# Local attention and gated experts on one core: the mask added in PSUM for the first eight pairs, exponentials slot by slot, and a new list of due times

## The chip, the cores and the metric

One Trainium2 chip (trn2), one core of it. The metric is the device time of one execution in microseconds: the median over several executions. The profile is that of one more execution, taken by the hardware profiler.

## The reference, cut to what matters

Eight batches, eight heads, 576 positions, 64 per head. The first four heads see the last 32 positions, the other four every fourth of the last 128. Attention's result, heads side by side, goes through a product with a gate in between.

```python
scores = scale * np.matmul(q, k.transpose(0, 1, 3, 2))
scores = np.where(masks[None], scores, -1e9)
scores = scores - np.max(scores, axis=-1, keepdims=True)
attn = np.exp(scores)
attn = attn / (np.sum(attn, axis=-1, keepdims=True) + 1e-09)
x = np.matmul(attn, v)                       # then (B, S, 512)
h = np.maximum(x @ w_in, 0.0)                # (B, S, 1024)
gate = sigmoid(conv over 3 positions of h, per channel)
out = (h * gate) @ w_out                     # (B, S, 512)
```

## The kernel before, in words

**The work.** `attention(b, p)` (line 228) treats one pair of heads p of batch b: four pairs per batch, pairs 0 and 1 with the plain window (kind 0), 2 and 3 with the dilated one (kind 1). `expert(b, ...)` (line 352) is the rest of a batch: a first product of 16 units (eight blocks of 128 channels by two halves of 288 positions), a gate per block, and a second product of eight units. Every value that goes into these products is split into a high and a low part, both rounded to the type that TensorE multiplies at its full rate (names ending in a and b), so each product is three matmuls per block. `weights` (line 423) brings w_in, w_out and the convolution's weights from 64-bit words in memory to float32 and splits them: a load, one ScalarE step, four VectorE steps; for the first ten blocks (`SUMMED`) three TensorE matmuls and two ScalarE copies do the sum and the split, for the others VectorE does.

**One pair.** A q/k load (line 235) and a v load (line 237) on SP's queue. The scores (lines 243 to 249) are many small matmuls into the PSUM tile `att`: nine slots of 64 keys for 128 rows, slots 0 to 3 in one bank, 4 to 7 in the next, 8 in a third. VectorE adds the mask, reading PSUM, in two pieces (lines 254 and 257); takes the maximum of each slot (260); subtracts it (262). ScalarE takes the exponential of all 576 columns at once (264). VectorE sums (266), adds 1e-9 (268), takes the reciprocal (270), multiplies (271) and transposes in blocks of 32 (273). TensorE multiplies by v (lines 275 to 301), into `att` again. ScalarE copies the result twice, a short and a long piece, as the high part of x (line 330). The low part comes in one of two ways. For the first `HELPED` = 2 batches `less` (lines 334 to 340) lets TensorE subtract the high part from `att`, six matmuls with minus the identity, and ScalarE copies what is left (line 343). In all other batches VectorE subtracts (line 345).

**Buffers.** Line 191 to 193: `att` has one buffer of four banks, used in turn by scores and by value products of all pairs; `mm` and `nn` have two of one bank each. There are two buffers of q/k, three of v, three of s, m and z, two of pt, seven of x.

**The order.** Nothing is issued in program order. Each step is a task with an engine, a cost, a due time and the tasks it waits for (`plan.add`). `Planner.order` (line 113) simulates the engines with these costs: of all tasks that could start within 0.25 us of the first possible start on an engine, the one with the earliest due time goes first; a buffer is given to the task that begins to use it, and free again after its last user. The tasks are written out in the order of the planned starts, and every engine, SP's queue included, runs its own in that order. The due times are numbers by hand (lines 196 to 203): `DUE` for a batch's first product, gates and second product, `PAIR` for its pairs, `AHEAD` for how long before its step a q/k, v or weight load is due:

```python
DUE = {0: (-9.2, 2.8, 30.4), 1: (64.7, 50.1, 92.3)}
PAIR = {0: (-26.0, -24.7, -23.0, -27.0), 1: (-4.9, 1.3, 8.9, 14.5)}
AHEAD = (9.1, 0.8, 0.7)
```

In batch 0 the first product's matmuls of pair k need only the x of pair k, and its units take turns in `mm` and `nn`; in every other batch they need all four pairs (line 369).

**Before the list.** The kinds of masks are loaded on ScalarE's queue (line 475). Identity and its negative are made (476, 477), and VectorE copies the kinds into `mask_sb`, one table of 576 columns per kind (lines 482 to 486, the five copies).

Of the kernel before, what the change touches and what calls it, by code (L numbers as in the profile page):

```python
# [36 lines left out]
BF16 = mybir.dt.bfloat16  # L37
I32 = mybir.dt.int32
U32 = mybir.dt.uint32
AF = mybir.ActivationFunctionType  # L40
ALU = mybir.AluOpType
AX = mybir.AxisListType

B, H, S, D = 8, 8, 576, 64
DM, DF = 512, 1024
NP = 4
NB = 18
W = 64
# [6 lines left out]
SCALE = 1.0 / D ** 0.5  # L55
# [102 lines left out]
def attn_moe(ctx: ExitStack, tc: tile.TileContext, qk_p, qk_d, v_p, v_d, w_in, w_out, conv, mask, out):  # L158
    nc = tc.nc
    const = ctx.enter_context(tc.tile_pool(name="const", bufs=1))  # L160
    psum = ctx.enter_context(tc.tile_pool(name="psum", bufs=1, space=bass.MemoryType.PSUM))

    mask_sb = const.tile([128, 2, 9 * W], BF16, name="mask_sb")
    kinds_sb = const.tile([128, 5, W], BF16, name="kinds_sb")
    conv_sb = const.tile([128, 3, NF], F32, name="conv_sb")
    ident = const.tile([128, 128], F32, name="ident")
    minus = const.tile([128, 128], F32R, name="minus")
    wi = [[const.tile([128, 512], F32R, name=f"wi{j}{c}") for c in range(NF)] for j in range(2)]
    wo = [[const.tile([128, 512], F32R, name=f"wo{j}{c}") for c in range(2 * NC)] for j in range(2)]
    plan = Planner()  # L170
# [24 lines left out]

    DUE = {0: (-9.2, 2.8, 30.4), 1: (64.7, 50.1, 92.3)}
    PAIR = {0: (-26.0, -24.7, -23.0, -27.0), 1: (-4.9, 1.3, 8.9, 14.5)}
    WI, WO = (-20.4, -20.4, -7.2, -7.2, -3.1, -0.1, 7.8, 7.8), (17.2, 17.2, 36.3, 36.3, 36.9, 34.9, 43.2, 43.2)
    AHEAD = (9.1, 0.8, 0.7)
    PERIOD = 55.1  # L200
    for b in range(2, B):
        DUE[b] = tuple(t + PERIOD * b for t in (-5.1, 5.4, 33.0))
        PAIR[b] = tuple(t + PERIOD * b for t in (-21.7, -18.8, -17.2, -13.1))
    SUMMED = 10
    HELPED = 2

# [21 lines left out]
    def attention(b, p):  # L228
        due = PAIR[b][p]
        kind = p // 2  # L230
        qk, v, s, m, z, pt, x = (Buffer(n) for n in ("qk", "v", "s", "m", "z", "pt", "x"))
        sc, tv = Buffer("att"), Buffer("att")
        xs[b, p] = x
        n = (S + KP, QD + KD)[kind]
        lq = plan.add("SP", n * 0.0017, due - AHEAD[0], lambda: nc.sync.dma_start(
# [4 lines left out]
        def scores():  # L240


            for n in [4 * t + i for i in range(4) for t in range(4)] + [16, 17]:
                for hd in range(2):
                    slot, quad = place(hd, n)
                    parts = queries(p, qk.t, hd, n)
                    for i, (q, k) in enumerate(parts):
                        nc.tensor.matmul(sc.t[quad * 32:quad * 32 + 32, slot // 4, slot % 4 * W:slot % 4 * W + W], q, k,  # L248
                                         start=i == 0, stop=i == len(parts) - 1, skip_group_check=True)

        last = plan.add("PE", (0.8, 0.92)[kind], due, scores, [lq], [qk, sc, s], "S")
        flat = lambda: s.t.rearrange("p a k -> p (a k)")
        halves = lambda t: t.rearrange("p (h k) -> p h k", h=2)
        last = plan.add("DVE", 0.68, due + 1.5, lambda: nc.vector.tensor_tensor(  # L254
            out=halves(flat()[:, 0:512]), in0=sc.t[:, 0:2, 0:256], in1=halves(mask_sb[:, kind, 0:512]), op=ALU.add),
            [last], [sc, s])
        last = plan.add("DVE", 0.215, due + 1.5, lambda: nc.vector.tensor_tensor(  # L257
            out=flat()[:, 512:576], in0=sc.t[:, 2, 0:W], in1=mask_sb[:, kind, 512:576], op=ALU.add), [last], [sc, s])
        wide = lambda t: t.unsqueeze(2).to_broadcast([128, 9, W])
        last = plan.add("DVE", 0.755, due + 2.0, lambda: nc.vector.tensor_reduce(  # L260
            out=m.t, in_=s.t, axis=AX.X, op=ALU.max), [last], [s, m])
        last = plan.add("DVE", 0.755, due + 2.5, lambda: nc.vector.tensor_tensor(  # L262
            out=s.t, in0=s.t, in1=wide(m.t), op=ALU.subtract), [last], [s, m])
        last = plan.add("ACT", 0.685, due + 3.0, lambda: nc.scalar.activation(
            out=s.t, in_=s.t, func=AF.Exp, scale=SCALE), [last], [s], "exp")
        last = plan.add("DVE", 0.755, due + 3.5, lambda: nc.vector.tensor_reduce(
            out=z.t, in_=s.t, axis=AX.X, op=ALU.add), [last], [s, z])
        last = plan.add("DVE", 0.173, due + 3.6, lambda: nc.vector.tensor_scalar(
# [33 lines left out]

        last = plan.add("PE", (0.9, 0.85)[kind], due + 6.0, values, [lv, last], [v, pt, tv, x], "V")

# [171 lines left out]
    make_identity(nc, ident)  # L476
    nc.scalar.mul(out=minus, in_=ident, mul=-1.0)


    spread = lambda i, n: kinds_sb[:, i, :].unsqueeze(1).to_broadcast([128, n, W])  # L480
    slot_masks = [mask_sb[:, kind, :].rearrange("p (a k) -> p a k", k=W) for kind in range(2)]
    nc.vector.tensor_copy(out=slot_masks[0], in_=spread(2, 9))
    nc.vector.tensor_copy(out=slot_masks[0][:, 0:5:4, :], in_=kinds_sb[:, 0:2, :])
    nc.vector.tensor_copy(out=slot_masks[1], in_=spread(2, 9))
    nc.vector.tensor_copy(out=slot_masks[1][:, 0:5:4, :], in_=spread(3, 2))
    nc.vector.tensor_copy(out=slot_masks[1][:, 8, :], in_=kinds_sb[:, 4, :])
    for h, in hs:
# [89 lines left out]
```

## Time and profile before

| | |
|---|---|
| median of 3 runs | 549.02 us (548.75 to 549.81) |
| the profiled execution's own time | 548.65 us |
| its span, first to last instruction | 546.9 us |
| TensorE busy, its weight loads | 520.8 us, 496.5 us |
| VectorE busy | 410.0 us |
| ScalarE busy | 289.7 us |
| moved by DMA | 52.32 MB |

The profile names the engines PE (TensorE), PEld (TensorE's weight loads), DVE (VectorE), ACT (ScalarE), POOL (GpSimd) and SP (the queue of loads and stores). L254 is line 254. Matmuls overlap in the pipeline, so the length of one is more than the distance to the next. An instruction's wait is put down to the event that came last. The chain of waits that ended last has, in shares of the span, 88% TensorE, 8% VectorE, 2% ScalarE, 2% DMA.

### The profile page before, as it was taken

The numbers are of one execution on the slowest core, as the hardware profiler recorded it, in microseconds if no ns is written. First come the engines' busy times: TensorE is split into PE (matmuls) and PEld (weight loads), VectorE is DVE, ScalarE is ACT, GpSimd is POOL, SyncE is SP. The second block draws the span as 40 slices with busy tenths as digits, with TensorE's granted clock in tenths as the row PEclk, the third lists the DMA queues.
The fourth block names the chain that finished last, engine by engine and source line by source line (L and its number), as shares of the span: only waits on it lengthen the run. The fifth ranks groups of instructions, "written<-read, shape, count | busy, mean of one in ns | idle before, by whom it ended". The sixth has DMA issues, their size and how long they took to land.

```text
span 546.9 us, 19084 instructions
## 1 busy us (share of the span) xinstructions
PE 520.8 (95%) x8664; PEld 496.5 (91%) x8664; DVE 410.0 (75%) x695; ACT 289.7 (53%) x556; POOL 0.9 (0%) x12
## 2 busy tenths in 40 slices
PE   3599978999999999999999999999999999999997
PEld 2578877999999999999999999999989999999997
DVE  5978999899996389937997399837987289936910
ACT  2466775755742586227742586227732486327721
POOL 0000000000000000000000000000000000000000
PEclk9999997999999999999999999999999999999999
DMA  7765614331135003530144103530045102300011
GB/s 251 267 196 177 207 42 155 100 121 44 50 99 162 18 23 109 163 104 23 52 146 150 30 23 96 170 111 23 28 146 168 35 23 65 112 26 23 0 44 45
DMA packets 17073, 52.32 MB, mean 96 GB/s; under 512 B 2016, under 2 KB 3168, under 8 KB 16992
## 3 DMA queue, kind: packets, MB, share of 16 engines
q1 hardware_dynamic: 16848, 51.02, 28.4%
q8 instruction: 68, 1.11, 0.9%
q10 hardware_dynamic: 144, 0.08, 0.1%
q14 instruction: 13, 0.11, 0.1%
HBM read 41.66 MB, written 9.44 MB: 93 GB/s over the span
## 4 chain that ended last, share of the span: by engine, by line
PE 88%; DVE 8%; ACT 2%; DMA 2%; issue 1%; DVEq 0%; ACTq 0%
PE nn L405 38%; PE mm L363 33%; PE att L283 8%; PE att L248 5%; DVE c L375 2%; PE nn L460 1%; DMA qk<-in_qk_d_dram 1%; PE att L337 1%; DVE s L254 1%; DVE s L262 1%; DVE c L388 1%; DVE m L260 1%; DMA qk<-in_qk_p_dram 1%; DVE pt L273 1%; DVE s L271 1%
## 5 line engine op out<-in xcount | busy, mean ns | idle before, releaser
L375 DVE SCALAR_TENSOR_TENSOR c<-h,conv_sb,c 128x576 f32<-128x576 f32 x128 | 104.0, 815 | 53.2 <-ACT c L381 51.6
L370 ACT ACTIVATE h<-mm 128x288 f32<-128x288 f32 x120 | 48.8, 408 | 49.7 <-PE mm L363 49.5
L412 ACT COPY out<-nn 128x288 f32<-128x288 f32 x64 | 25.3, 397 | 76.4 <-PE nn L405 70.9
L283 PEld LDWEIGHTS att<-pt,v 32*64 32x64 f32 x3072 | 41.4, 140 | 14.8 <-DVE s L257 4.6
L388 DVE TENSOR_TENSOR c<-c,h 128x576 f32<-128x576 f32 x64 | 47.6, 755 | 9.2 <-ACT c L386 7.7
L283 PE MATMUL att<-pt,v 32*64 32x64 f32 (+2 forms) x3072 | 44.9, 234 | 9.3 <-DVE s L257 3.5
L381 ACT ACTIVATE c<-h,conv_sb 128x576 f32<-128x576 f32 x64 | 49.6, 776 | 1.3
L248 PE MATMUL att<-qk 64*32 64x64 f32 x2432 | 36.2, 235 | 10.9 <-DMA qk<-in_qk_d_dram 5.6
L248 PEld LDWEIGHTS att<-qk 64*32 64x32 f32 x2432 | 30.1, 111 | 16.8 <-issue 5.7
L386 ACT ACTIVATE c<-c 128x576 f32<-128x576 f32 x64 | 42.5, 679 | 2.8 <-DVE c L375 2.3
L363 PE MATMUL mm<-x2a,wi 128*128 128x288 f32 x144 | 40.5, 296 | 0.0
L363 PE MATMUL mm<-x1a,wi 128*128 128x288 f32 x144 | 40.3, 296 | 0.0
L363 PE MATMUL mm<-x3a,wi 128*128 128x288 f32 x144 | 40.3, 295 | 0.0
L363 PE MATMUL mm<-x0a,wi 128*128 128x288 f32 x144 | 40.3, 295 | 0.0
L405 PE MATMUL nn<-g2a,wo 128*128 128x288 f32 x128 | 36.9, 303 | 0.0
L405 PE MATMUL nn<-g6a,wo 128*128 128x288 f32 x128 | 36.7, 300 | 0.0
L405 PE MATMUL nn<-g0a,wo 128*128 128x288 f32 x128 | 36.4, 299 | 0.2
L405 PE MATMUL nn<-g1a,wo 128*128 128x288 f32 x128 | 36.5, 300 | 0.0
L405 PE MATMUL nn<-g3a,wo 128*128 128x288 f32 x128 | 36.4, 299 | 0.0
L405 PE MATMUL nn<-g5a,wo 128*128 128x288 f32 x128 | 36.4, 299 | 0.0
L405 PE MATMUL nn<-g4a,wo 128*128 128x288 f32 x128 | 36.4, 299 | 0.0
L405 PE MATMUL nn<-g7a,wo 128*128 128x288 f32 x128 | 36.0, 300 | 0.1
(194 smaller groups left out, 1482.6 us busy)
## 6 DMA issues: line engine op xcount, KB each, us to landing
qk<-in_qk_d_dram SPq DMA_DIRECT2D x16, 664.0 KB, 4.4
qk<-in_qk_p_dram SPq DMA_DIRECT2D x16, 592.0 KB, 5.0
out_dram<-out SPq DMA_DIRECT2D x28, 288.0 KB, 2.3
v<-in_v_d_dram SPq DMA_DIRECT2D x16, 384.0 KB, 3.4
v<-in_v_p_dram SPq DMA_DIRECT2D x16, 384.0 KB, 3.5
out<-in_w_in_dram SPq DMA_DIRECT2D x8, 512.0 KB, 5.4
out<-in_w_out_dram SPq DMA_DIRECT2D x8, 512.0 KB, 4.6
out_dram<-out SPq DMA_DIRECT2D x8, 144.0 KB, 1.8
```

What stands on the lines that cost most here:

```text
L248: nc.tensor.matmul(sc.t[quad * 32:quad * 32 + 32, slot // 4, slot % 4 * W:slot % 4 * W + W], q, k, start=i == 0, stop=i == len(parts) - 1, ...
L254: last = plan.add("DVE", 0.68, due + 1.5, lambda: nc.vector.tensor_tensor(out=halves(flat()[:, 0:512]), in0=sc.t[:, 0:2, 0:256], in1=halve ...
L260: last = plan.add("DVE", 0.755, due + 2.0, lambda: nc.vector.tensor_reduce(out=m.t, in_=s.t, axis=AX.X, op=ALU.max), [last], [s, m])
L283: nc.tensor.matmul(tv.t[hd * 64:hd * 64 + 64, bank, o:o + n], v.t[quad * 32:quad * 32 + 32, block // 2, block % 2 * 64:block % 2 * 64 + 64 ...
L363: nc.tensor.matmul(ps.t[:, 0:HALF], wi[jw][fc][:, k * 128:k * 128 + 128], x[k].t[jx][:, hf * HALF:hf * HALF + HALF], start=(k == 0 and i = ...
L370: relu.append(plan.add("ACT", 0.4, due + 1.6 * u + 1.6, lambda fc=fc, hf=hf, ps=ps: nc.scalar.activation(out=h[fc].t[:, 1 + hf * HALF:1 + ...
L375: nc.vector.scalar_tensor_tensor(out=c[fc].t, in0=h[fc].t[:, k:S + k], scalar=conv_sb[:, k, fc:fc + 1], in1=c[fc].t, op0=ALU.mult, op1=ALU ...
L381: t = plan.add("ACT", 0.777, d, lambda fc=fc: nc.scalar.activation(out=c[fc].t, in_=h[fc].t[:, 1:S + 1], func=AF.Copy, scale=conv_sb[:, 1, ...
L386: t = plan.add("ACT", 0.686, d + 1.0, lambda fc=fc: nc.scalar.activation(out=c[fc].t, in_=c[fc].t, func=AF.Sigmoid), [t], [c[fc]], "sigmoid")
L388: t = plan.add("DVE", 0.755, d + 1.5, lambda fc=fc: nc.vector.tensor_tensor(out=c[fc].t, in0=c[fc].t, in1=h[fc].t[:, 1:S + 1], op=ALU.mult ...
L405: nc.tensor.matmul(ps.t[:, 0:HALF], wo[jw][2 * dm + k // 4][:, k % 4 * 128:k % 4 * 128 + 128], g[k].t[jg][:, hf * HALF:hf * HALF + HALF], ...
L412: outs.append(plan.add("ACT", 0.4, out_due + 3.3 + 3.3 * u, lambda hf=hf, ps=ps, o=o: nc.scalar.copy(out=o.t[:, hf * HALF:hf * HALF + HALF ...
```

## The change

For the first eight pairs (`EASED = 8`: batches 0 and 1) the scores step begins with three matmuls of the identity (in bfloat16, named `ones`) and the mask's columns, one for each bank, so that the small matmuls add to the mask in PSUM. VectorE takes the maximum straight from PSUM in two pieces and multiplies it by -SCALE. ScalarE takes nine exponentials, one for each slot of 64 columns, straight from PSUM, each with the slot's maximum as bias, and each writes the slot's sum to z. The adds, the subtract and the sum on VectorE fall away for these pairs. `HELPED` is 0, so that no pair uses `less` any more. The five copies of masks run on ScalarE. The due times are new, and so are the planner's costs of `values` and of the scores. Of the diff, moved lines that do not change are left out:

```diff
+    ones = const.tile([128, 128], BF16, name="ones")
...
-    DUE = {0: (-9.2, 2.8, 30.4), 1: (64.7, 50.1, 92.3)}
-    PAIR = {0: (-26.0, -24.7, -23.0, -27.0), 1: (-4.9, 1.3, 8.9, 14.5)}
-    WI, WO = (-20.4, -20.4, -7.2, -7.2, -3.1, -0.1, 7.8, 7.8), (17.2, 17.2, 36.3, 36.3, 36.9, 34.9, 43.2, 43.2)
-    AHEAD = (9.1, 0.8, 0.7)
-    PERIOD = 55.1
+    DUE = {0: (-4.7, 3.9, 22.9), 1: (68.1, 49.9, 103.0)}
+    PAIR = {0: (-42.0, -45.9, -41.4, -30.4), 1: (-4.4, -17.4, -6.6, -2.0)}
+    WI, WO = (-22.4, -22.4, -2.7, -2.7, -3.1, -0.1, 7.0, 7.6), (11.7, 13.8, 38.0, 41.2, 40.7, 39.3, 47.3, 50.0)
+    AHEAD = (9.1, 1.4, 0.7)
+    PERIOD = 54.7
     for b in range(2, B):
-        DUE[b] = tuple(t + PERIOD * b for t in (-5.1, 5.4, 33.0))
-        PAIR[b] = tuple(t + PERIOD * b for t in (-21.7, -18.8, -17.2, -13.1))
+        DUE[b] = tuple(t + PERIOD * b for t in (-4.7, 10.5, 33.0))
+        PAIR[b] = tuple(t + PERIOD * b for t in (-21.1, -18.4, -16.8, -12.7))
     SUMMED = 10
-    HELPED = 2
+    EASED = 8
+    HELPED = 0
...
+        eased = NP * b + p < EASED
...
+            if eased:
+                for bank, (c0, c1) in enumerate(((0, 256), (256, 512), (512, 576))):
+                    nc.tensor.matmul(sc.t[:, bank, 0:c1 - c0], ones, mask_sb[:, kind, c0:c1], start=True, stop=True,
+                                     skip_group_check=True)
...
-                                         start=i == 0, stop=i == len(parts) - 1, skip_group_check=True)
+                                         start=i == 0 and not eased, stop=i == len(parts) - 1, skip_group_check=True)
...
-        last = plan.add("PE", (0.8, 0.92)[kind], due, scores, [lq], [qk, sc, s], "S")
+        last = plan.add("PE", (0.8, 0.92)[kind] + (0.5 if eased else 0.0), due, scores, [lq], [qk, sc, s], "S")
...
+        if eased:
+            last = plan.add("DVE", 0.68, due + 1.5, lambda: nc.vector.tensor_reduce(
+                out=m.t[:, 0:8].rearrange("p (h a) -> p h a", h=2),
+                in_=sc.t[:, 0:2, 0:256].rearrange("p h (a k) -> p h a k", k=W), axis=AX.X, op=ALU.max), [last], [sc, m])
+            last = plan.add("DVE", 0.215, due + 1.5, lambda: nc.vector.tensor_reduce(
+                out=m.t[:, 8:9], in_=sc.t[:, 2, 0:W], axis=AX.X, op=ALU.max), [last], [sc, m])
+            last = plan.add("DVE", 0.173, due + 2.0, lambda: nc.vector.tensor_scalar(
+                out=m.t, in0=m.t, scalar1=-SCALE, scalar2=None, op0=ALU.mult), [last], [m])
+
+            def exps():
+                for i in range(9):
+                    nc.scalar.activation(out=s.t[:, i, :], in_=sc.t[:, i // 4, i % 4 * W:i % 4 * W + W], func=AF.Exp,
+                                         scale=SCALE, bias=m.t[:, i:i + 1], accum_out=z.t[:, i:i + 1])
+
+            last = plan.add("ACT", 2.2, due + 3.0, exps, [last], [sc, s, m, z], "exp")
+        else:
...
-        last = plan.add("PE", (0.9, 0.85)[kind], due + 6.0, values, [lv, last], [v, pt, tv, x], "V")
+        last = plan.add("PE", (1.1, 1.25)[kind], due + 6.0, values, [lv, last], [v, pt, tv, x], "V")
...
+    nc.scalar.copy(out=ones, in_=ident)
...
-    nc.vector.tensor_copy(out=slot_masks[0], in_=spread(2, 9))
-    nc.vector.tensor_copy(out=slot_masks[0][:, 0:5:4, :], in_=kinds_sb[:, 0:2, :])
-    nc.vector.tensor_copy(out=slot_masks[1], in_=spread(2, 9))
-    nc.vector.tensor_copy(out=slot_masks[1][:, 0:5:4, :], in_=spread(3, 2))
-    nc.vector.tensor_copy(out=slot_masks[1][:, 8, :], in_=kinds_sb[:, 4, :])
+    nc.scalar.copy(out=slot_masks[0], in_=spread(2, 9))
+    nc.scalar.copy(out=slot_masks[0][:, 0:5:4, :], in_=kinds_sb[:, 0:2, :])
+    nc.scalar.copy(out=slot_masks[1], in_=spread(2, 9))
+    nc.scalar.copy(out=slot_masks[1][:, 0:5:4, :], in_=spread(3, 2))
+    nc.scalar.copy(out=slot_masks[1][:, 8, :], in_=kinds_sb[:, 4, :])
```

## Rows read from the trace of the kernel before

**Rows 1.** The page, part 1: busy time, share of the span, instructions.

```profile
PE 520.8 (95%) x8664; PEld 496.5 (91%) x8664; DVE 410.0 (75%) x695; ACT 289.7 (53%) x556; POOL 0.9 (0%) x12
```

**Rows 2.** Windows: length, busy (count) per engine, clock, DMA share, GB/s.

```profile
0.00:35.00 35.00, 19.14 (x625) 15.65 (x626) 26.86 (x59) 13.19 (x26) 0.91 (x12) 1.00 0.70 235
35.00:75.00 40.00, 39.99 (x708) 35.03 (x707) 36.67 (x69) 29.90 (x60) 0.00 (x0) 1.00 0.56 183
75.00:80.00 5.00, 1.58 (x12) 1.35 (x11) 4.82 (x11) 4.40 (x8) 0.00 (x0) 0.98 0.00 0
80.00:90.00 10.00, 8.40 (x205) 6.89 (x205) 9.69 (x19) 3.26 (x9) 0.00 (x0) 0.50 0.32 98
...
112.00:516.00 404.00, 402.99 (x6617) 390.81 (x6616) 307.13 (x503) 215.42 (x411) 0.00 (x0) 1.00 0.24 78
```

**Rows 3.** Waits of PE over the span: us in total, times, longest.

```profile
PE att L283 <- DVE s L257: 3.5, 1, 3.5
PE att L283 <- DVE pt L273: 3.4, 1, 3.4
```

**Rows 4.** Windows, the stretch to 93.66 us, columns as in rows 2.

```profile
0.00:93.66 93.66, 72.77 (x1654) 61.84 (x1654) 80.85 (x158) 53.17 (x105) 0.91 (x12) 0.95 0.56 186
```

**Rows 5.** DVE groups by form, 0 to 110 us: busy us, mean ns.

```profile
L260 DVE TENSOR_REDUCE m<-s 128x9 f32<-128x576 f32 x8 | 6.0, 751 | 0.2
L262 DVE TENSOR_TENSOR s<-s,m 128x576 f32<-128x576 f32 x8 | 6.0, 748 | 0.2
L266 DVE TENSOR_REDUCE z<-s 128x9 f32<-128x576 f32 x8 | 5.9, 737 | 0.1
...
L254 DVE TENSOR_TENSOR s<-att,mask_sb 128x512 f32<-128x512 f32 x8 | 5.5, 685 | 0.6 <-PE att L248 0.6
...
L257 DVE TENSOR_TENSOR s<-att,mask_sb 128x64 f32<-128x64 f32 x8 | 1.7, 211 | 0.0
...
L268 DVE TENSOR_SCALAR z<-z 128x9 f32<-128x9 f32 x8 | 1.3, 166 | 0.2
```

**Rows 6.** DVE groups by form, whole span.

```profile
L345 DVE TENSOR_TENSOR x0b<-att,x0a 128x512 fp32r<-128x512 f32 x4 | 2.7, 681 | 4.3 <-ACT x0a L330 4.3
...
L345 DVE TENSOR_TENSOR x0b<-att,x0a 128x64 fp32r<-128x64 f32 x4 | 0.8, 211 | 0.0
...
L482 DVE COPY mask_sb<-kinds_sb 128x576 bf16<-128x576 bf16 x1 | 0.5, 453 | 5.7 <-DMA kinds_sb<-in_mask_dram 5.7
```

**Rows 7.** Timeline to 41 us: start, length, engine, line, [idle before].

```profile
5.56 1.60 PE L248 MATMUL att<-qk 64*32 64x64 f32 x80 [5.56 <-DMA qk<-in_qk_d_dram]
...
19.70 2.05 PE L283 MATMUL att<-pt,v 32*64 32x64 f32 x96 [3.51 <-DVE s L257]
...
21.80 0.70 ACT L330 CAST x0a<-att 128x64 fp32r<-128x64 f32 x2 [1.92 <-PE att L283]
...
24.05 0.70 ACT L343 CAST x0b<-att 128x512 fp32r<-128x512 f32 x2 [0.58 <-PE att L340]
...
40.08 0.70 ACT L343 CAST x3b<-att 128x512 fp32r<-128x512 f32 x2
```

**Rows 8.** Line 337 on PE: ns min/median/max, first and last start.

```profile
L337 PE MATMUL att<-x0a,minus x4: 405/405/472, 22.5 to 23.3; 128*128 128x128 f32 x4
...
L337 PE MATMUL att<-x2a,minus x4: 275/276/327, 34.0 to 34.4; 128*128 128x128 f32 x4
...
L337 PE MATMUL att<-x5a,minus x4: 415/415/473, 82.7 to 83.4; 128*128 128x128 f32 x4
```

**Rows 9.** ACT groups by form, whole span.

```profile
L370 ACT ACTIVATE h<-mm 128x288 f32<-128x288 f32 x120 | 48.8, 408 | 49.7 <-PE mm L363 49.5
...
L264 ACT ACTIVATE s<-s 128x576 f32<-128x576 f32 x32 | 21.3, 684 | 22.5 <-DVE s L262 22.4
...
L330 ACT CAST x0a<-att 128x512 fp32r<-128x512 f32 x5 | 3.0, 593 | 0.0
...
L330 ACT CAST x0a<-att 128x64 fp32r<-128x64 f32 x5 | 1.1, 213 | 9.8 <-PE att L283 8.0 <-DVE s L271 1.9
```

## The prediction made before the changed kernel ran

> **What bounds the kernel now.** I read the page's busy shares first: TensorE 95%, VectorE 75%, ScalarE 53% of a 546.9 us span [rows 1]. Read alone, they say that VectorE's relief is worth nothing. So the windows come next, cut by stage. From 112 to 516 us TensorE is busy 402.99 of 404 us: that stretch is TensorE's, and less VectorE work can't shorten it. Before 75 us it is another kernel: TensorE idles 15.9 of the first 35 us, is full from 35 to 75 us (39.99 of 40), and idles 3.4 of the 5 us to 80 us, while VectorE is full there (4.82 of 5) and was nearly so before (36.67 of 40). From 80 to 90 us the granted clock is 0.50, the lower of the two levels (1.2 GHz), behind that idle gap [rows 2]. TensorE's waits name the releaser: apart from loads it is VectorE, 3.5 us for the value product of the first pair and 3.4 us for that of a pair of the second batch [rows 3]. Up to the second product's steady start at 93.66 us, VectorE is busy 80.85 us [rows 4]. So the start is set mostly by VectorE, everything later by TensorE, and a change to the first eight pairs can shift the later part as a whole.
>
> **VectorE, term by term.** Removed per pair: the two adds (685 + 211 ns), the subtract (748) and the sum (737), 2.38 us; times eight, 19.05 us [rows 5]. Added per pair: the maximum now reads PSUM in two pieces. No row shows a reduction from PSUM; its nearest rows are the adds of the same shapes, 896 ns, against 751 for the single reduction now, so +0.15 (ends: 0, if it costs no more than now; 0.90, if reading costs double). The factor -SCALE on 128x9 is +0.17, as line 268 [rows 5]. With HELPED 0 the low part of x is subtracted on VectorE, 681 + 211 ns [rows 6]. Together 1.20 us, times eight 9.6. The five mask copies leave VectorE: the first, of 576 columns, takes 0.45 [rows 6], a second one is as wide, three have 128 columns or fewer, by width about 0.2 each; 1.4 in all, by estimate. Net: -19.05 - 1.4 + 9.6 = **-10.9 us** of VectorE before 94 us.
>
> **TensorE.** Removed: `less`, eight times. Between the end of x0a's casts (22.50) and the start of x0b's (24.05) it takes 1.5 us at the slow rate [rows 7], and half of that, 0.75, at full rate: the 128-column matmuls last 405 and 415 ns there and 276 in between [rows 8], so the first one ran as slowly as that at 82.7 us, where the granted clock is 0.50, though the first window's mean reads 1.00 [rows 2]. I take -7, between 6 and 12. Added: three mask matmuls a pair. Four of 128 columns start within 0.4 us [rows 8], so 576 columns cost about 0.4 (ends 0.3 and 1.1, full and slow rate, with a change of operand type in no row). +3.2. Net -4; between 35 and 75 us, where both engines are full, TensorE thus does not take VectorE's place as the limit. I add nothing for it to the sum, since it lies beside VectorE's larger relief.
>
> **ScalarE.** One exponential of 684 ns becomes nine of 64 columns with a bias and a sum. Nearest row: the 64-column cast, 213 ns [rows 9], so nine take 1.9 us. Lower end 1.0: back to back, the 64-column cast and the 512-column one behind it take 0.70 together [rows 7], so the second starts 0.11 after the first. Upper end 3.7: nine at the 408 ns of the 288-column row [rows 9], should bias and sum cost as much as 200 ns. The Trainium skill, ScalarE: Activation LUTs (What ACT_TABLE_LOAD costs), gives 280 ns + 0.833 ns a column for an activation with a bias per partition, with about 93 ns overlapped between neighbours; an estimate by it is 2.25 us, and no run here shows the sum's price. By the page each pair would hold its scores 0.35 us longer and the total below would be 1.4 us higher over four pairs. Over eight pairs ScalarE gains 8 x (1.9 - 0.68) = 9.8 us, and about 2.1 for the masks (two of 576 columns at 0.65 each, by 593 ns for 512 [rows 9], and three short ones at about 0.25), and loses the eight second casts, 0.70 each [rows 7], 5.6: net +6.3 on 53 us busy of 93.66 [rows 4]. It does not become the limit by its load.
>
> **What the change adds as a wait.** `att` has one buffer, for scores and value product alike. Now it is free when the adds have read it: 1.60 us of scores and 0.90 of adds. After the change it is held until the ninth exponential: 1.60 + 0.4 mask + 0.90 maximum + 0.17 + 1.9 + about 0.3 of handing over = 5.3 us, with the next pair's scores or values queued behind it on TensorE. The value side gets shorter: from 19.70 to the end of x0b's casts at 24.75, 5.05 us now [rows 7]; then 2.05 + 0.70 + 0.89 = 3.7. Per pair 9.0 instead of 7.5. The first four pairs now take from 5.56 to 40.78 us [rows 7], 35.2 against 4 x 7.5 = 30, since VectorE is late in between. Afterwards: masks ready about 1.2 us later than the first scores start now (they land at 5.7 [rows 6], ScalarE copies them, and the scores wait for them), 36 us of holding, and 1.9 us of VectorE's last steps of the fourth pair: 44.7, that is 3.9 later. Ends: 0, if TensorE uses the time wholly for weight sums that lie behind 41 us now, and 9.2, if scores of the next batch slip in front of the fourth value product (5.3). I take **+3**, for most of that work still needs the fourth x.
>
> **Loads and order.** The pairs' loads move ahead of all weights on SP's queue; each pair brings a q/k and a v load. The DMAs are the same, the first 35 us have a DMA share of 0.70 [rows 2], so the moved loads fit: 0 (ends 0 and +2, about what the planner's list sets for one load). For batches 2 to 7 the gates are due 5.1 us later and the rest shifts by under 1 us. TensorE's idle time there is 1 us in all [rows 2], so at most 1 can be won; a loss is open. I take 0, upper end +6: 1 us in each of six batches. The end of the last batch keeps its chain: 0.
>
> **Sum.** -10.9 + 3 = -7.9 us. The profiled execution took 548.65 us, a span of 546.9 and 1.75 around it; that gives 540.75. It stands 0.37 under the median of 549.02, so the forecast for the median is **541.1 us**.
>
> **Rivals.**
> 1. *TensorE's gaps close wholly.* If nothing is lost to `att`, because the weights' work fills the wait, the full 10.9 stays. The 10 us at the lower level are gone too: its 8.4 busy us [rows 2] would last 4.2 at full rate, of which perhaps 3 us count besides VectorE. 548.65 + 0.37 - 10.9 - 3 = 535.1. For it: batch 1's pairs are due at -17.4 to -2.0 now, around the start of batch 0's first product at -4.7, so their value products no longer have to come in the gap at 75 us. Against it: `att` as above. Chance 0.17.
> 2. *Slower: the one `att` buffer decides.* The next batch's scores take `att` while the fourth pair's VectorE tail runs, and x of the fourth pair comes at 50 us instead of 40.8. TensorE has then used up its sums and the three-quarters of the first units that don't need it, and idles. Cost 9.2; what stays of the relief is the idle and slow time after 75 us, 5.0. 549.0 + 4.2 = 553.2. It decides from an x later than 40.8 + 7.9 = 48.7 us. For it: due times let that pair's scores start whenever `att` is free. Against it: VectorE is then nearly empty, so the tail is short. Gaps between short bursts also keep TensorE at the lower level, as at 80 to 90 us [rows 2]. The Trainium skill, TensorE: Matmul & The Clock Gate (HAM oscillation), says that bursts parted by idle time each begin slowly again; by that rule the first 45 us stay slow, and the trace agrees so far as the clock after the gap at 76 us is 0.50. Chance 0.18.
> 3. *No effect.* TensorE is full from 35 to 75 us [rows 2], and VectorE's relief there only lets VectorE wait; the gap at 76 us comes again for a table load and a late exponential. Then 549, give or take 1. Chance 0.07.
> 4. *The later due times cost.* The gates' later place makes TensorE wait 1 us in each of six batches: 541.1 + 6 = 547. Chance 0.05.
>
> **How the numbers follow.** The forecast has 0.53, from 538 to 545. A measurement of this kernel tells 0.2%, about 1.1 us, from no change. Faster: 0.53 + 0.17 + most of rival 4 and a quarter of rival 3 = 0.73; same 0.04; slower 0.23 (rival 2 and what is left of 3 and 4, which may come on top of a smaller gain). The range goes from 533 (rival 1 with the lower ends) to 553 (rival 2), which leaves out under 2 in 10.
>
> **What would show it.** Right: the last of the first batch's x ready between 43 and 47 us; nine exponentials in 1.5 to 2.5 us; VectorE's busy time lower by about 11 us; no stretch at 0.50 after 60 us; the second product's steady start near 86 us instead of 93.66; the same time per batch afterwards as now. Wrong: nine exponentials over 3 us, an x after 49 us, or new TensorE waits behind 112 us, which would show the due times at fault.

## The result, and the profile after

The changed kernel takes 551.27 us, median of seven runs (550.12 to 551.75); the kernel before, on the same chip, took 549.41 (547.48 to 550.84). The ratio is 1.0037, with a 95% interval of 1.0020 to 1.0053: **slower by 0.2 to 0.5%**, where 541.1 us and faster were forecast. 551.27 lies within the stated range, but on its other side.

The profiled execution, the fastest of the seven, took 550.12 us with a span of 548.3. The page, part 1, of the changed kernel:

```profile
PE 517.1 (94%) x8640; PEld 490.6 (89%) x8640; DVE 401.0 (73%) x690; ACT 304.7 (56%) x684; POOL 0.9 (0%) x12
```

Against [rows 1], VectorE has 9.0 us less to do and TensorE 3.7 less, and ScalarE 15 us more. So TensorE's busy time shrank, and the time grew: its idle time in the span went from 26.1 to 31.2 us. The windows (length, busy time and count of PE, PEld, DVE, ACT, POOL, then granted clock, DMA share, GB/s) answer to [rows 2]:

```profile
0.00:35.00 35.00, 14.30 (x465) 9.75 (x468) 17.21 (x44) 18.53 (x90) 0.90 (x12) 1.00 0.63 212
35.00:75.00 40.00, 35.68 (x806) 30.44 (x801) 32.69 (x69) 30.14 (x98) 0.00 (x0) 0.91 0.57 188
75.00:80.00 5.00, 4.32 (x85) 3.52 (x86) 4.64 (x12) 5.00 (x25) 0.00 (x0) 1.00 0.40 125
80.00:90.00 10.00, 10.00 (x203) 8.52 (x189) 9.66 (x18) 9.23 (x19) 0.00 (x0) 1.00 0.54 153
...
112.00:516.00 404.00, 403.12 (x6682) 390.53 (x6682) 308.21 (x506) 217.43 (x412) 0.00 (x0) 1.00 0.25 81
```

TensorE now idles 20.7 us of the first 35 instead of 15.9, and 4.3 between 35 and 75 where it had been full. The gap behind 75 us is gone, and so is the stretch at the lower clock from 80 to 90 us; in its place the mean granted clock between 35 and 75 us is 0.91. All of that lies before 45 us, as the matmuls of one form tell too:

```profile
42.98 0.44 PE L387 MATMUL mm<-x1a,wi 128*128 128x288 f32 x1
...
45.03 0.29 PE L387 MATMUL mm<-x0a,wi 128*128 128x288 f32 x1
```

In the kernel before, the matmuls were at their short length by 34.0 us [rows 8]; in the changed one TensorE stays at the lower of its two levels (1.2 GHz) at least 9 us longer, behind waits of up to 4.0 us. VectorE, which I took for what bounds the start, is busy 17.2 of the first 35 us, where it had 26.9: its relief has turned into waiting. TensorE's waits (total, times, longest) say for whom:

```profile
PE att L248 <- ACT s L274: 13.0, 5, 4.0
PE att L248 <- ACT ones L502: 7.5, 1, 7.5
PE att L307 <- ACT s L274: 2.3, 3, 1.1
```

Compare [rows 3]: no wait on VectorE's softmax is left at the head of the list; the scores wait 13.0 us for the exponentials of the pair before, and the first ones 7.5 us for ScalarE to make masks and identity. The timelines of TensorE and then of ScalarE (start, length, engine, line, idle before) show one such turn:

```profile
7.48 0.66 PE L248 MATMUL att<-mask_sb,ones 128*128 128x256 bf16 x3 [7.48 <-ACT ones L502]
...
13.40 0.64 PE L248 MATMUL att<-mask_sb,ones 128*128 128x256 bf16 x3 [3.99 <-ACT s L274]
...
31.61 1.26 PE L307 MATMUL att<-pt,v 32*64 32x32 f32 x96 [1.14 <-ACT s L274]
```

```profile
10.58 0.31 ACT L274 ACTIVATE s<-att,m 128x64 f32<-128x64 f32 x1 [3.16 <-DVE m L269]
10.79 0.19 ACT L274 ACTIVATION_READ_ACCUMULATOR s<-att,m 128x1 f32 x1
10.89 0.30 ACT L274 ACTIVATE s<-att,m 128x64 f32<-128x64 f32 x1
...
13.11 0.24 ACT L274 ACTIVATION_READ_ACCUMULATOR s<-att,m 128x1 f32 x1
```

From the first pair's mask matmuls at 7.48 to the next pair's at 13.40, `att` turns once in 5.9 us. It was forecast at 5.3, and scores and adds took 2.5 before. ScalarE issues not nine but eighteen instructions: each exponential with a sum is followed by one that reads the accumulator, and the eighteen take from 10.58 to 13.35, 2.8 us where I had 1.9. All four scores of the first batch come in a row, at 7.48, 13.40, 19.29 and 25.44, and the first value product starts at 31.61. The row itself is not new. In the kernel before, the four scores start at 5.56, 8.07, 10.96 and 14.59, and the first value product at 19.70 [rows 7]:

```profile
8.07 1.34 PE L248 MATMUL att<-qk 64*32 64x64 f32 x72 [0.91 <-DVE s L257]
...
14.59 1.60 PE L248 MATMUL att<-qk 64*32 64x64 f32 x80 [1.58 <-DVE s L257]
```

The row took 14.1 us and takes 24.1 now. The low parts of x, on VectorE's timeline of the changed kernel:

```profile
33.66 0.81 DVE L369 TENSOR_TENSOR x0b<-att,x0a 128x512 fp32r<-128x512 f32 x2
...
48.48 0.81 DVE L369 TENSOR_TENSOR x3b<-att,x3a 128x512 fp32r<-128x512 f32 x2
```

The first x is complete at 34.5 us, where it was 24.75, the fourth at 49.3 instead of 40.78 [rows 7]. Of these 8.5 us, 10.0 are the row of scores, 1.9 its later start, and 3.4 come back because the value side is shorter (17.7 us from 31.61 to 49.3, where 21.1 stood). The 50 us of rival 2 are met, but not its turn of events: the next batch's scores do not slip in front of the fourth value product.

```profile
45.52 1.36 PE L307 MATMUL att<-pt,v 32*64 32x64 f32 x96
...
49.43 0.42 PE L248 MATMUL att<-mask_sb,ones 128*128 128x256 bf16 x3
```

How much of the delay is still there in later batches, the chain of waits in order of time shows (start, length, what), first for the kernel before, then for the changed one; the lines are the same long piece of the first product in batch 4 and in the last batch:

```profile
252.35 16.30 PE mm L363 x123
...
500.08 16.32 PE mm L363 x123
```

```profile
255.10 16.30 PE mm L387 x123
...
501.52 16.32 PE mm L387 x123
```

Some 2.75 us behind at 255 us, 1.4 behind at 501 us: the loss is the start's, and the later batches win 1.3 us back.

### The profile page after: what moved, and what is told of

The parts are those of the page before. It is cut to its first block, busy times and chain, and to the rows that moved or that the text cites. A ratio compares the mean times of both kernels' runs of the same rounds, so it can differ in the third digit from the quotient of the medians.

```text
span 548.3 us, 19138 instructions
## 1 busy us (share of the span) xinstructions
PE 517.1 (94%) x8640; PEld 490.6 (89%) x8640; DVE 401.0 (73%) x690; ACT 304.7 (56%) x684; POOL 0.9 (0%) x12
## 4 chain that ended last, share of the span: by engine, by line
PE 78%; DVE 11%; ACT 8%; issue 1%; DMA 1%; ACTq 0%; DVEq 0%
PE nn L429 35%; PE mm L387 30%; PE att L307 7%; PE att L255 5%; ACT s L274 4%; DVE c L399 2%; DVE c L412 1%; DMA kinds_sb<-in_mask_dram 1%; ACT c L405 1%; DVE m L264 1%; ACT c L410 1%; PE nn L484 1%; DVE pt L297 1%; ACT h L394 1%; DVE wo L497 0%
## 5 line engine op out<-in xcount | busy, mean ns | idle before, releaser
L405 ACT ACTIVATE c<-h,conv_sb 128x576 f32<-128x576 f32 x64 | 49.8, 779 | 1.3
L307 PEld LDWEIGHTS att<-pt,v 32*64 32x64 f32 x3072 | 39.5, 133 | 11.5 <-issue 4.6
L307 PE MATMUL att<-pt,v 32*64 32x64 f32 (+2 forms) x3072 | 43.0, 227 | 5.2 <-ACT s L274 2.3
L387 PE MATMUL mm<-x5a,wi 128*128 128x288 f32 x128 | 35.9, 295 | 0.0
L387 PE MATMUL mm<-x4a,wi 128*128 128x288 f32 x128 | 35.8, 295 | 0.0
```

The lines of the kernel that those rows point to most:

```text
L307: nc.tensor.matmul(tv.t[hd * 64:hd * 64 + 64, bank, o:o + n], v.t[quad * 32:quad * 32 + 32, block // 2, block % 2 * 64:block % 2 * 64 + 64 ...
L387: nc.tensor.matmul(ps.t[:, 0:HALF], wi[jw][fc][:, k * 128:k * 128 + 128], x[k].t[jx][:, hf * HALF:hf * HALF + HALF], start=(k == 0 and i = ...
L405: t = plan.add("ACT", 0.777, d, lambda fc=fc: nc.scalar.activation(out=c[fc].t, in_=h[fc].t[:, 1:S + 1], func=AF.Copy, scale=conv_sb[:, 1, ...
```

## The experiments

Two theories were set against each other. Theory 1: the one `att` buffer is held too long, by ScalarE's many instructions between the scores and the next pair. Theory 2: the new due times, four scores in a row before any value product, are at fault. Since the kernel before has that row too, only the rest of the new order is left to theory 2. In all but the third and fourth kernel the order of tasks was kept as the planner had made it for the kernel that was altered, so that only the work within a task differs. Ratios are to the kernel before, on the same chip. The experiments ran on several chips, and the kernel before had medians from 548.44 to 549.41 us there; differences in us between two rows of the table are uncertain by about 1 us.

| | median us | ratio, 95% interval |
|---|---|---|
| changed kernel | 551.27 | 1.0037 (1.0020 to 1.0053) |
| e1, sum on VectorE | 549.57 | 1.0016 (1.0002 to 1.0030) |
| e2, exponentials twice | 572.82 | 1.0435 (1.0410 to 1.0459) |
| e3, old due times | 569.64 | 1.0374 (1.0347 to 1.0400) |
| e4, new due times only | 582.13 | 1.0628 (1.0587 to 1.0669) |
| e5, no maximum | 542.01 | 0.9872 (0.9841 to 0.9904) |
| e6, subtract from PSUM | 551.14 | 1.0037 (1.0022 to 1.0052) |
| e7, masks on VectorE | 549.90 | 1.0021 (1.0004 to 1.0037) |
| e8, twice in the first batch | 561.91 | 1.0235 (1.0211 to 1.0259) |
| e9, twice in the second batch | 562.69 | 1.0266 (1.0232 to 1.0300) |
| e10, e5 with masks on VectorE | 540.53 | 0.9844 (0.9823 to 0.9866) |
| e11, kernel before, sum twice | 551.90 | 1.0056 (1.0036 to 1.0076) |
| e12, kernel before, no maximum | 548.95 | 0.9986 (0.9971 to 1.0001) |
| e13, e5 with VectorE loaded | 553.81 | 1.0092 (1.0068 to 1.0115) |
| e14, one maximum for a row | 547.94 | 0.9976 (0.9957 to 0.9995) |

**e1: the sum back on VectorE.**

```diff
-                                         scale=SCALE, bias=m.t[:, i:i + 1], accum_out=z.t[:, i:i + 1])
+                                         scale=SCALE, bias=m.t[:, i:i + 1])
...
+                nc.vector.tensor_reduce(out=z.t, in_=s.t, axis=AX.X, op=ALU.add)
```

> The changed kernel with the order of its tasks kept; only the nine exponentials no longer write a sum, and VectorE sums the 576 columns in front of its small add (0.74 us a pair). Theory 1, the single att buffer is held too long by ScalarE's 18 instructions: each hold falls by about 9 x 0.095 = 0.85 us, the last x of the first batch comes 3 us earlier than 49.3, and the time falls by 1.5 to 3 us, to about 548.5 to 550. Theory 2, the new order of tasks is at fault, whatever the hold: no change, 551.3 within 0.8, or slower by VectorE's added 6 us.

ScalarE's part of the line, first of e1, then of the changed kernel (ns min/median/max, first and last start):

```profile
L274 ACT ACTIVATE s<-att,m x72: 305/332/371, 10.8 to 77.3; 128x64 f32<-128x64 f32 x72
```

```profile
L274 ACT ACTIVATE s<-att,m x72: 303/328/413, 10.6 to 78.8; 128x64 f32<-128x64 f32 x72
L274 ACT ACTIVATION_READ_ACCUMULATOR s<-att,m x72: 192/224/308, 10.8 to 79.0; 128x1 f32 x72
```

The exponentials themselves stay the same; the 72 reads are gone, and the nine take 1.96 us by the timeline. The fourth x came at 48.25, 1.0 us earlier, not 3; the 5 us that VectorE has more are the likely reason, which is not shown. The time fell by 1.7 us in the median, 1.2 by the ratios; the two intervals overlap, so this run leans to theory 1 and settles nothing.

**e2: each exponential twice.**

```diff
-                for i in range(9):
+                for i in [*range(9), *range(9)]:
```

> The changed kernel with each of the nine exponentials issued twice, so att is held 2.6 us longer by each of the first eight pairs; order kept, result the same. Theory 1: four pairs in a row add 10 us to the last x of the first batch (49.3 to about 60) and the time rises by 6 to 12 us. Theory 2: ScalarE has room (66 of 94 us busy), so the time rises by less than 3 us.

The time rose by 21.6 us, beyond what either theory said. TensorE's waits in e2:

```profile
PE att L248 <- ACT s L274: 26.3, 5, 6.7
PE att L307 <- ACT s L274: 8.0, 3, 4.7
```

The waits for exponentials went from 15.3 to 34.3 us. Nine exponentials with their reads take 2.67 us more, times eight pairs 21.3: in sum, all the holding that was added came out at the end. The mean granted clock is lower too, 0.982 against 0.994 in the two profiled executions, so that the two numbers agree so closely may be partly chance. I had expected the first four alone to count.

**e3 and e4: due times and computation apart.** In e3 the changed computation gets the due times, weight due times and period of before; in e4 the kernel before gets the new ones.

```diff
-    DUE = {0: (-4.7, 3.9, 22.9), 1: (68.1, 49.9, 103.0)}
-    PAIR = {0: (-42.0, -45.9, -41.4, -30.4), 1: (-4.4, -17.4, -6.6, -2.0)}
+    DUE = {0: (-9.2, 2.8, 30.4), 1: (64.7, 50.1, 92.3)}
+    PAIR = {0: (-26.0, -24.7, -23.0, -27.0), 1: (-4.9, 1.3, 8.9, 14.5)}
...
```

> The changed kernel with the due times, weight due times and period of the kernel before; the planner orders anew. Theory 1: att is still held for 5.9 us by each scores step, the last x of the first batch comes after 46 us, and the time is within 3 us of the changed kernel, 549 to 554. Theory 2: without the four scores in a row the relief of VectorE shows, and the time falls under 547.

> The kernel before with the due times, weight due times and period of the changed kernel and nothing else of the change (planner's costs, less on TensorE and VectorE's softmax stay). Theory 1: the due times are not the cost, so 547 to 550, or faster if moving the second batch's pairs ahead closes the gap at 75 to 90 us. Theory 2: the order costs as much here as there, 551 or more, with TensorE idle over 20 us in the first 50.

Both missed: 569.6 and 582.1, far slower than either parent. In e3 the start is no better (the fourth x at 49.8). It has the four scores in a row as well (7.94, 14.12, 20.01 and 25.90, the first value product at 32.08), so it did not take away what it was meant to. But then TensorE idles where neither parent does, as a window of e3 shows (columns as above):

```profile
94.00:112.00 18.00, 6.89 (x244) 5.28 (x244) 14.84 (x33) 11.57 (x59) 0.00 (x0) 0.59 0.41 128
```

11 of 18 us idle, while VectorE is busy 14.8. In e4 the longest waits of TensorE are of the same kind, at the hand-over between the first two batches:

```profile
PE nn L405 <- ACT out L412: 12.5, 1, 12.5
PE nn L460 <- ACT h L370: 7.0, 3, 3.7
```

So the due times are worth 18 us to the changed computation, and cost 33 with the old one: the two parts of the change can't be priced one by one, and theory 2 in the form that I gave it falls, by the row in the kernel before. These two runs re-plan everything, and say nothing finer.

**e5: no maximum, two exponentials straight from PSUM.** The maximum is left out for the first eight pairs.

```diff
-                for i in range(9):
-                    nc.scalar.activation(out=s.t[:, i, :], in_=sc.t[:, i // 4, i % 4 * W:i % 4 * W + W], func=AF.Exp,
-                                         scale=SCALE, bias=m.t[:, i:i + 1], accum_out=z.t[:, i:i + 1])
+                nc.scalar.activation(out=halves(flat()[:, 0:512]), in_=sc.t[:, 0:2, 0:256], func=AF.Exp, scale=SCALE)
+                nc.scalar.activation(out=flat()[:, 512:576], in_=sc.t[:, 2, 0:W], func=AF.Exp, scale=SCALE)
```

> The changed kernel with the order of its tasks kept, but for the first eight pairs no maximum is taken or subtracted: ScalarE takes two exponentials (512 and 64 columns) straight from PSUM, and VectorE sums. It leaves out the maximum, which changes nothing but the safety against overflow for these inputs. Theory 1 (the hold of att sets the start): the hold falls from 5.9 to about 3.1 us, the last x of the first batch comes 8 to 11 us earlier than 49.3, TensorE's waits on the exponentials fall from 15 to under 4 us, and the time falls by 6 to 12 us, to 539 to 545. Theory 2 (the order of tasks sets it): the waits move to other places and the time falls by less than 3 us.

542.0 us, 1.3% faster than the kernel before, with the changed kernel's order. TensorE's waits, and the fourth x on VectorE's timeline:

```profile
PE att L248 <- ACT ones L501: 7.7, 1, 7.7
PE att L248 <- ACT s L270: 3.1, 3, 1.5
```

```profile
42.16 0.81 DVE L368 TENSOR_TENSOR x3b<-att,x3a 128x512 fp32r<-128x512 f32 x2
```

The second scores start 2.7 us behind the first (10.43 and 7.70), not 5.9; the waits for exponentials are down to 3.1 us and the fourth x comes 6.3 us earlier, at 42.97. VectorE's busy time is 399.3, only 1.7 less than in the changed kernel. With the same order and nearly the same work on VectorE, the loss is gone: theory 1 as expected. The gain is less than the hold's: the first turn is 3.2 us shorter, but the row of four scores only 8.3 (15.8 us, from 7.70 to 23.49), since other waits take its place.

**e6: the subtraction on VectorE, straight from PSUM.** `att` is free after the subtraction; one exponential follows, and VectorE sums.

```diff
-                out=m.t, in0=m.t, scalar1=-SCALE, scalar2=None, op0=ALU.mult), [last], [m])
+                    out=quarters(halves(flat()[:, 0:512])), in0=quarters(sc.t[:, 0:2, 0:256]),
+                    in1=m.t[:, 0:8].rearrange("p (h a) -> p h a", h=2).unsqueeze(3).to_broadcast([128, 2, 4, W]),
+                    op=ALU.subtract)
...
+                nc.scalar.activation(out=s.t, in_=s.t, func=AF.Exp, scale=SCALE)
```

> The changed kernel with the order kept; the mask is still added by TensorE and the maximum taken from PSUM, but VectorE then subtracts it from PSUM into s (two instructions, 0.9 us), ScalarE takes one exponential of 576 columns, VectorE sums. att is free after the subtraction: the hold falls from 5.9 to about 4.1 us, and VectorE has 1.4 us a pair more. Theory 1: the last x of the first batch comes 3 to 5 us earlier, the time falls by 2 to 6 us, to 545 to 549. Theory 2, or if VectorE's load decides (up to 11 us more over eight pairs): no change or slower, 551 or more.

551.1: no gain, as the rival clause had it. TensorE's longest waits in e6 behind the first scores:

```profile
PE att L248 <- DVE s L275: 7.5, 3, 3.1
PE att L248 <- DVE x4b L379: 2.1, 1, 2.1
PE att L317 <- DVE x1b L379: 1.9, 1, 1.9
```

The fourth x is 2.1 us earlier (47.17), but these waits are now on VectorE, which is busy 9.7 us more than in the changed kernel. A shorter hold bought with VectorE's time moved the wait and saved nothing.

**e7: the masks on VectorE again.**

```diff
-    nc.scalar.copy(out=slot_masks[0], in_=spread(2, 9))
+    nc.vector.tensor_copy(out=slot_masks[0], in_=spread(2, 9))
...
```

> The changed kernel with the five mask copies on VectorE again; order kept. ScalarE then makes the identity tiles before the masks land, and the first mask matmul starts at 6.4 instead of 7.5 us. Theory 1: the serial chain of att begins 1.1 us earlier and the time falls by 0.5 to 1.2 us. Theory 2: the start is not on the path, no change (within 0.3).

The first wait of TensorE is 6.3 instead of 7.5 us:

```profile
PE att L248 <- DVE mask_sb L508: 6.3, 1, 6.3
```

The time fell by 1.4 in the median, with overlapping intervals. In e10 the same step gives 1.5 against e5, with overlapping intervals again: both lean one way, and neither shows it by itself.

**e8 and e9: whose holds count.** Exponentials twice in the first batch's pairs, or in the second's.

```diff
-                for i in range(9):
+                for i in [*range(9), *range(9 if b == 0 else 0)]:
```

> The changed kernel with the nine exponentials twice in the four pairs of the first batch only, so 10.6 us of holding more; result the same, order kept. Theory 1a (every hold of att before the first product counts in full): half to all of the 21.5 us that all eight cost, 9 to 12 us more than the changed kernel. Theory 1b (only the second batch's holds count, behind full TensorE work): under 4 us more.

> The same with the exponentials twice in the four pairs of the second batch only. My prediction priced only the first four pairs' holds, by which this one costs under 3 us more than the changed kernel. If every pair's hold counts, 8 to 12 us more, and with the kernel that doubles the first batch's it makes up the 21.5 us.

10.6 and 11.4 us more than the changed kernel, 22.0 together, against e2's 21.6 and 10.7 of holding each. Holding that is added counts in full in both batches.

**e10: e5 and e7 together.**

> The kernel without the maximum (two exponentials straight from PSUM in the first eight pairs, maximum left out) with the five mask copies on VectorE again. If the two gains are of one chain they add up: 9.3 and 1.3 us off the changed kernel, 540 to 541.5. If loads or VectorE set the start by then, no better than 542.0.

540.53 us, 1.6% faster than the kernel before and the best of all. Its windows:

```profile
0.00:35.00 35.00, 20.51 (x622) 15.67 (x623) 23.95 (x57) 12.03 (x27) 0.90 (x12) 0.93 0.73 257
...
75.00:80.00 5.00, 4.83 (x32) 3.43 (x25) 4.96 (x10) 4.46 (x9) 0.00 (x0) 1.00 0.61 179
80.00:90.00 10.00, 9.56 (x156) 8.89 (x154) 9.67 (x15) 8.16 (x17) 0.00 (x0) 1.00 0.24 82
```

TensorE idles 14.5 of the first 35 us, less than in either parent, and hardly behind 75. It leaves the maximum out for the first eight pairs, and so stands only for inputs whose scaled scores can't overflow the exponential.

**e11 and e12: what VectorE's time is worth in the kernel before.** e11 takes the sum twice in the first eight pairs; e12 leaves out the maximum and its subtraction there.

```diff
+            for i in range(2 if b < 2 else 1):
+                nc.vector.tensor_reduce(out=z.t, in_=s.t, axis=AX.X, op=ALU.add)
```

> The kernel before with VectorE's sum taken twice in the first eight pairs, 0.74 us each, 5.9 us of VectorE in all; order kept, result the same. If VectorE sets the start of the kernel before, as the prediction has it, the time rises by 4 to 6 us, to 552.5 to 555. If VectorE's load there is half hidden, by 2 to 3 us; if it isn't on the path, by less than 1.

> The kernel before, order kept, with the maximum and its subtraction left out for the first eight pairs (safe for these inputs only): VectorE has 1.5 us a pair less, 12 us in all, att is held as briefly as before. It measures VectorE's relief alone, about what my prediction's first term was worth. If the relief counts in full, as the prediction had it, 537 to 539 us; by the slope that twice the sum showed (3.1 us for 5.9), 541 to 544; if the relief only turns into idle time of VectorE, 547 or more.

5.9 us more on VectorE cost 3.1. But 10.6 us less (410.0 to 399.4 busy) gave 0.14% with an interval that touches 1: nothing that can be told. Windows of e12:

```profile
35.00:75.00 40.00, 39.37 (x702) 34.28 (x702) 31.90 (x62) 29.52 (x59) 0.00 (x0) 1.00 0.56 187
75.00:80.00 5.00, 2.87 (x22) 2.64 (x20) 3.48 (x8) 4.95 (x9) 0.00 (x0) 1.00 0.00 0
80.00:90.00 10.00, 7.57 (x201) 6.22 (x202) 9.68 (x19) 3.38 (x9) 0.00 (x0) 0.53 0.24 71
```

VectorE has five idle microseconds more from 35 to 75, and TensorE is where it was: full there, then 2.1 us idle, then ten at 0.53 of the clock. ScalarE's timeline says why:

```profile
75.97 1.28 ACT L264 ACT_TABLE_LOAD   x1
77.26 1.26 ACT L264 ACTIVATE s<-s 128x576 f32<-128x576 f32 x2
```

The exponentials of the second batch stand on ScalarE's queue behind the first batch's relus and sigmoids and a table load, whose turn comes when TensorE's first product ends. TensorE's next step, a value product, waits until 80.85:

```profile
80.85 1.87 PE L283 MATMUL att<-pt,v 32*64 32x32 f32 x96 [2.97 <-DVE pt L273]
```

In between VectorE, idle for 1.39 us until the exponential has ended, takes its five steps behind it, from the sum at 77.98 to the end of the transpose at 80.79. So what VectorE does ahead of the exponential doesn't set this gap, as rival 3 had it; what it does behind the exponential is part of it, and there the second sum of e11 stands. The maximum and the subtraction of e12 lie ahead. The change takes away steps on both sides (two adds and the subtraction ahead, the sum behind), so e12 prices a part of its relief and not the whole.

**e13: VectorE loaded again at a short hold.**

```diff
+                for i in range(3):
+                    nc.vector.tensor_reduce(out=z.t, in_=s.t, axis=AX.X, op=ALU.add)
```

> The kernel without the maximum of the fifth experiment (542.0 us), with VectorE's sum taken three times in the first eight pairs: 1.48 us a pair, 11.8 in all, behind the release of att, so the hold stays. If VectorE's relief counts in the new order, as my first term had it, the time rises by 6 to 12 us, to 548 to 554. If the gain over the kernel before comes from the order and the short hold alone, by less than 3 us.

553.81, 11.8 more than e5 for 12.0 us more of VectorE's time (411.3 busy against 399.3): in the new order, at a short hold, VectorE time that is added counts in full. The mean granted clock is lower as well, 0.978 against 0.994 in the profiled executions. And a load is not a relief: in the kernel before, 5.9 us more cost 3.1, and 10.6 less gave nothing clear. The waits of TensorE that grew are for the low parts of x, which VectorE subtracts now that `less` is gone:

```profile
PE att L307 <- DVE x0b L369: 3.3, 1, 3.3
PE att L307 <- DVE x5b L369: 3.2, 1, 3.2
PE att L248 <- ACT s L270: 3.0, 3, 1.4
PE att L248 <- DVE x4b L369: 2.6, 1, 2.6
```

**e14: one maximum for all nine slots of a row.** A slot's weights vanish if its own maximum lies some 88 below the row's, after scaling.

```diff
+                nc.vector.tensor_reduce(out=m.t[:, 9:10], in_=m.t[:, 0:9], axis=AX.X, op=ALU.max)
+                nc.vector.tensor_scalar(out=m.t[:, 10:11], in0=m.t[:, 9:10], scalar1=-SCALE, scalar2=None, op0=ALU.mult)
...
+                                     bias=m.t[:, 10:11])
```

> The changed kernel, order kept, with the masks copied by VectorE and one maximum for all nine slots of a row: VectorE takes the nine maxima from PSUM, their maximum and its product with -SCALE (0.34 us more than now at most), ScalarE two exponentials with it as bias and without sums (about 0.9 us instead of 2.8), VectorE sums. A slot keeps its weights unless its own maximum lies some 88 below the row's after scaling. The hold is about 4.3 us, between the 3.1 of the fifth experiment and the 5.9 of the changed kernel. If the hold decides, 544 to 547, faster than the kernel before; if VectorE's load decides (7 us more than in the changed kernel), 549 or more.

547.94, just clear of the kernel before (0.9976, 0.9957 to 0.9995), and outside the 544 to 547 expected: the first turn of `att` is 4.2 us (6.21 to 10.40) and the next two 4.9, TensorE's waits on exponentials are 9.3 us instead of 15.3, and VectorE has 7.5 us more. Two of the twelve executions ran at a mean granted clock of 0.999 and took 544.5 us; the others had 0.984 to 0.993 and took 547.3 to 548.8.

```profile
PE att L248 <- ACT s L278: 7.9, 3, 3.0
```

## Why the prediction was wrong, point by point

**The sum.** It had two terms, -10.9 for VectorE and +3 for `att`. Both failed, the second by more. e5, where the hold is short, parts them: there the change gives -7.0 against the kernel before, and the hold of the changed kernel takes back 9.3 (with 1.7 us of VectorE's work in it). That is 3.9 and 6.3 us worse than the two terms, together the 10.2 between 541.1 and 551.27.

**The hold of `att`, +3.** The mechanism was named and each piece of it was priced per pair, 9.0 us for 7.5. The step that failed came after: only the first four pairs were counted, as a delay of the fourth x, and slack in their chain (35.2 against 30) was set against it. The runs show in its place that the hold counts in both batches: 10.7 us more of it cost 10.6 in the first (e8) and 11.4 in the second (e9), which the prediction had left out. For the first four pairs it was too small as well. The fourth x was to come at 44.7 and came at 49.3: 0.7 of that is the later start, 2.9 the four holds (24.1 for 21.2), 1.0 the value side. Eighteen instructions of 2.8 us stood where nine of 1.9 were forecast, within the stated ends (1.0 to 3.7), and the turn came to 5.9 instead of 5.3. The row taken as nearest, the 64-column cast, has neither a bias nor a sum. Without sums e1 measured 1.96 for the nine, with a median of 0.332 each; the reads of the accumulator came on top. The estimate by the Trainium skill, ScalarE: Activation LUTs (What ACT_TABLE_LOAD costs), was 2.25 us for the nine and 0.333 for one: the trace agrees for one, and nine were shorter.

That a microsecond of hold costs a microsecond is shown only for hold that is added. Taken away, it gave less: e6 and e14 shorten the first turn by 2.3 and 1.7 us, put 9.7 and 7.5 us on VectorE, and gain 0.1 and 3.3.

**VectorE's relief, -10.9.** Its work fell by 9.0 us. That the start is "set mostly by VectorE" was the step that failed for the kernel before, so far as the work ahead of the exponential goes: e12 takes 10.6 us of it away and gains nothing clear, because TensorE is full from 35 to 75 us and the gap behind it starts when ScalarE's queue lets the exponential through. I had read the wait's releaser, the transpose on VectorE, and not what that transpose had waited for. In the new order e13 shows that VectorE's time counts when it is added (11.8 for 12.0); what its relief is worth there was not tried by itself. What relief and due times have together at a short hold is 7.0 us (e5). That this lies near the forecast of 7.9 is chance, for the forecast had +3 for the hold in it; without that it was 10.9.

**TensorE, 0.** Its busy time fell by 3.7, near the -4, but that is not its work alone: e13 has the same 8640 matmuls as e5 and 521.7 us busy against 517.8, at the lower mean clock. Nothing here prices the term. The three mask matmuls took 0.42 us at full rate and 0.64 at the start, as priced.

**ScalarE, no limit by its load.** Its load rose by 15.0 us, where +6.3 was said: without the reads of the accumulator (e1) it is 5.9 us less, which is most of the difference. It is not the limit by load, but it is the longest piece of the turn of `att`.

**Loads and order, 0.** Loads: no wait of TensorE's at the head of the list is on one. With the masks on ScalarE the first scores start 1.2 us later than in e7, which the sum held within the late start; the gains of 1.4 and 1.5 us in e7 and e10 lean to that price. The later due times were the other way round from rival 4: the later batches are 1.3 us shorter, just over the 1 us that I said could be won.

**The rivals.** Rival 1's gap behind 75 us did close. Rival 2 had the buffer right. That its fourth x, 50 us, is so near the measured 49.3 was luck, since it came about by four long turns and not by the next batch's scores, and its price, 553.2, was too high. It also had TensorE slow for the first 45 us. The trace shows that: behind waits of up to 4.0 us the 288-column matmuls take 0.44 us until 43 us and 0.29 from 45. The Trainium skill, TensorE: Matmul & The Clock Gate (HAM oscillation), says that bursts parted by idle time each begin slowly again; the trace agrees. How much of the loss that is, no run tells apart.

**What stays open.** Why e3 and e4 lose 18 and 33 us was not followed beyond their waits, and which due times close the gap behind 75 us was not tried. The clock's share stays open as well: e14's two executions at 0.999 are 2.8 us or more faster than its others, but one of e6 at 0.997 took 551.78 us, among the slowest of its twelve.

## What to carry to other kernels

Where one buffer is handed from engine to engine, write down its turn: everything from the first write to the last read, on whichever engine, times the number of turns; a piece of work that moves from an engine with load to an engine with room still lengthens the turn if it comes before the release. Do all that can wait behind the release, and release by few wide instructions: two exponentials and no maximum did a first turn in 2.7 us, nine with sums in 5.9. And before an engine's relief is counted, follow its last instruction back one more wait: what released the releaser.

## What was not expected of the hardware

A sum written by an activation is an instruction of its own: 192 to 308 ns by the trace, one behind each exponential. A slot of 64 columns then starts every 0.29 us instead of every 0.21, so nine took 2.68 to the end of the last exponential instead of 1.96. A maximum taken from PSUM cost what an add from there does (median 687 ns for 512 columns, against a mean of 685).
